# Key sums ahead of the routing, q's transpose ahead of the gates, three place steps a piece: one table of orders changed in a one-core kernel

## The chip, the core and the metric

The program runs on one core of a Trainium2 chip. The metric is the device time of one execution in microseconds (us), as the median of several. Five engines work side by side, each through its own queue in order: TensorE (PE in the profile: matmuls and transposes; PEld are its weight loads), VectorE (DVE), ScalarE (ACT), GpSimd (POOL) and SyncE (SP, which here issues most DMAs).

## What is computed

Attention with keys and values averaged over eight neighbours, then a mixture of experts in two levels, where each token goes to one of 4 x 4 experts:

```
k_p = k.reshape(B, H, Sp, pool, D).mean(axis=3)        # B, H, S, D = 8, 8, 576, 64; pool 8
v_p = v.reshape(B, H, Sp, pool, D).mean(axis=3)
attn = softmax(scale * q @ k_p^T); x = attn @ v_p      # x: 4608 tokens of 512
...
g_idx = np.argmax(x @ w_group, axis=1)                 # group of a token
e_idx = np.argmax(xg @ w_expert[g], axis=1)            # expert in the group
h = np.maximum(xg[mask_e] @ w1[g, e], 0.0)
out[tok_idx] = combined[:, None] * (h @ w2[g, e])      # combined: product of the two softmax weights
```

With the inputs given, seven of the eight batches send all 576 tokens to one expert; batch 5 sends 20 tokens elsewhere.

## The kernel before

The kernel takes the batches b = 0 to 7 one after the other. In the body of batch b, TensorE runs the expert (class `Moe`, `m` in the plans) on batch b: 16 pieces `m.up:f:half` (12 matmuls each, line L532; relu on ScalarE into `ht`, L534; the low-order part `m.upd` on VectorE, L539), then 14 pieces `m.down` of 8 matmuls (L553, L563), whose results ScalarE scales into `y` and stores. All 576 tokens go to the batch's main expert, the one with most tokens. Every float32 operand is used as a high and a low part, so each weight is split: ScalarE casts it (L517), GpSimd, or VectorE where the plan says `:v`, subtracts (L518).

Between these pieces the body does the attention of batch b+1 (`n`, class `Att`), and the start of batch b+2 (`x`): loads of k, v and q, key sums `kr` (L208, two of them), the sum of the rest `rr` (L214), `kb` and `krz` on ScalarE (L226, L227), which TensorE transposes in `kt` (L263, L268); q's transpose on VectorE `qb` (L285); scores `sc` (L291). The sums of v are three folds on GpSimd, `vr` (L230 to L232), then `vmain`: a cast (L245) and four activations (L249) on ScalarE and a subtraction on GpSimd (L246). Loads of k and v share three buffers, so v's second load (`load_v:1`, L176) needs the first key sum done. The bodies 1 to 6 follow the plan STEADY; `x` exists in the bodies 1 to 5. FIRST is the body of batch 0, LAST that of batch 7.

The routing (`n.rt`, `n.route`, `n.main_expert`) turns x into logits `lt` (L371, copied by ScalarE in two halves, L372), transposes them (L379), and finds the expert of each token in 16 short VectorE instructions (L382 to L406) that end in the one-hot `oh`. TensorE counts it (L412), and the expert with most tokens goes to a SyncE register, which the next weight loads use (L510). `gates` (L469 to L483) makes the tokens' weights, `keep_x` (L488 to L494) stores x to DRAM if a token of the batch is left over.

Left-over tokens (class `Left`, `l`) are done at the end in blocks of 32: `place` yields 18 steps that give each a place (`l.step` runs the next one; L621 to L656), `which` finds the block's batch and expert (L663 to L673), `slots` and `rows` its tokens (L678 to L703), `fetch_x`, `fetch_a`, `fetch_b` load x and the weights, `turn` transposes x, `gather`, `back`, `up`, `hback` and `down` do the expert. The first block stands in LAST between the pieces of batch 7; further ones would be done by the loop `block` after it.

What sets the order: a plan is a string of pieces, run from left to right. TensorE, SyncE and VectorE execute in the order of the plan (`MANUAL`; in START all five engines do); the order on ScalarE and GpSimd is set by the framework's planner, from its own model of durations, so a plan that is rearranged can reorder these two as well.

Of the kernel before, what the change touches and what calls it, by code (L numbers as in the profile page):

```python
# [13 lines left out]
ALU = mybir.AluOpType  # L14
# [11 lines left out]
CH = [(0, 128), (128, 128), (256, 128), (384, 128), (512, 64)]  # L26
# [39 lines left out]
x.load_qb:2 x.load_qb:3 x.load_v:0 m.up:6:0 m.upd:6:0 m.split:2:3 m.up:6:1 m.upd:6:1 n.px_:4 n.pm:4 n.pxd:4 n.pmd:4 m.up:7:0 m.upd:7:0  # L66
m.up:7:1 m.upd:7:1 n.av:0:0:256 n.avd:0:0:256 n.av:1:0:256 n.avd:1:0:256 n.av:2:0:256 n.avd:2:0:256 n.av:3:0:256 n.avd:3:0:256
n.av:0:256:320 n.avd:0:256:320 n.av:1:256:320 n.avd:1:256:320 n.av:2:256:320 n.avd:2:256:320 n.av:3:256:320 n.avd:3:256:320 n.rt:0:256
m.down:0 n.rt:256:320 m.down:1 n.route m.down:2 m.down:3 n.main_expert w.load:1:0 w.load:1:1 w.load:1:2 w.load:1:3 m.down:4 x.kr:0 x.kr:1
x.rr x.rcopy x.kb x.load_v:1 m.down:5 n.gates n.keep_x m.down:6 x.vr:0 x.vr:1 m.down:7 w.split:1:0 w.load:2:0 x.kt x.qb:0 m.down:8 m.down:9  # L70
w.split:1:1 w.load:2:1 x.sc:0 x.mx:0 x.sb:0 x.qb:1 m.down:10 x.vmain x.vrem m.down:11 x.su_:0 x.nm:0:p m.down:12 m.down:13
"""
LAST = """
m.up:0:0 m.upd:0:0 m.split:1:2 m.load:2:2 l.step l.step m.up:0:1 m.upd:0:1 l.step l.step m.up:1:0 m.upd:1:0 m.split:1:3 m.load:2:3 l.step
l.xtiles l.step m.up:1:1 m.upd:1:1 l.step l.step m.up:2:0 m.upd:2:0 m.split:2:0 l.step l.step m.up:2:1 m.upd:2:1 l.step l.step m.up:3:0 m.upd:3:0
m.split:2:1:v l.step l.step m.up:3:1 m.upd:3:1 l.step l.step m.up:4:0 m.upd:4:0 l.step l.step m.up:4:1 m.upd:4:1 m.split:2:2 l.step l.step
m.up:5:0 m.upd:5:0 l.tiles l.which l.fetch_x l.fetch_a:1 l.fetch_b:1 m.up:5:1 m.upd:5:1 m.up:6:0 m.upd:6:0 m.split:2:3 m.up:6:1 m.upd:6:1
m.up:7:0 m.upd:7:0 l.slots m.up:7:1 m.upd:7:1 m.down:0 m.down:1 l.rows m.down:2 m.down:12 m.down:13 m.down:3 l.turn:0 l.turn:2
l.turn:1 m.down:4 l.turn:3 l.turn:4 l.next_ l.fetch_x m.down:5 l.gather m.down:6 l.back m.down:7 l.up l.fetch_a m.down:8 l.hback l.slots m.down:9
l.down l.rows l.fetch_b m.down:10 m.down:11  # L80
"""
MANUAL = [{ET.PE, ET.SP, ET.DVE, ET.Activation, ET.Pool}, {ET.PE, ET.SP, ET.DVE}, {ET.PE, ET.SP, ET.DVE}]

# [2 lines left out]
def attn_moe(ctx: ExitStack, tc: tile.TileContext, q, k, v, wg, we, w1, w2, out):  # L86
    nc = tc.nc
# [485 lines left out]
    class Left:  # L573
# [151 lines left out]
        def fetch_b(s, first=None):  # L725
            for j in range(4):
                nc.sync.dma_start(out=s.wb[j], in_=w2v[bass.ds(s.re, 1), :, 2 * j:2 * j + 2, :].rearrange("o p k f -> p (o k) f"),
                                  **({} if first else dict(cond=s.some)))

        def turn(s, c):  # L730

            if s.xr is None:
                s.xr = xp.tile([128, 2, 4, S], F32, name="xt").rearrange("p i g s -> p (i g s)")[:, 0:NC * DM].rearrange("p (c x) -> p c x", c=NC)
            o, n = CH[c]
            ps = ps_t.tile([128, 512], F32, name="tp")
            (nc.gpsimd if c % 2 else nc.vector).tensor_tensor(
                out=s.xh[0][:, :, o:o + n], in0=s.xh[0][:, :, o:o + n], in1=s.xh[1][:, :, o:o + n], op=ALU.add)
# [51 lines left out]
            s.which()  # L789

        def block(s):
            for c in range(NC):
                s.turn(c)
            s.next_()
            s.fetch_x()
            s.gather()
            s.back()
            s.up()
            s.fetch_a()
            s.slots()  # L800
            s.rows()
            s.hback()
            s.down()
            s.fetch_b()
# [67 lines left out]
```

## Time and profile before

| | us |
|---|---|
| median of 3 runs (632.47 to 637.88) | 632.96 |
| the profiled execution, whole / its span | 632.83 / 631.1 |
| TensorE busy in the span | 592.0 |
| VectorE / ScalarE / GpSimd busy | 428.3 / 282.4 / 254.4 |
| TensorE's granted clock, mean (1.00 is 2.4 GHz, .50 is 1.2 GHz) | 0.989 |

A row of a timeline gives the start, the duration, the engine, the line, the operation, output<-inputs by the program's names, the partitions x elements, how many were merged (xcount), and in brackets how long the engine was idle before it and what released it. A duration includes time in which the instruction was held. Lines are those of the kernel before; in the changed kernel the lines from about L730 on stand 3 or 4 further down.

### The profile page before, as it was taken

To read this page: it belongs to the slowest core of one execution; us is meant where nothing else is said; L and a number is where in the kernel's file an instruction comes from. 1 tells how busy PE (TensorE), PEld (TensorE's weight loads), DVE (VectorE), ACT (ScalarE), POOL (GpSimd) and SP (SyncE) were. 2 spreads that over 40 slices of the span, in tenths; PEclk is the share of its full clock that TensorE was granted. 3 is DMA by queue.
4 is the path that set the end of the run, shared out by engine and by line. 5 is a ranking of instruction groups with operands and counts; after the bars stand their busy time and mean duration, and the time that the engine had idled before them with its cause. 6 is when DMAs were issued, how large, how long until landed. Compare 5 with 4: busy or idle time off the path is not lost.

```text
span 631.1 us, 10875 instructions
## 1 busy us (share of the span) xinstructions
PE 592.0 (94%) x3851; PEld 526.9 (83%) x3851; DVE 428.3 (68%) x1002; ACT 282.4 (45%) x585; POOL 254.4 (40%) x255
## 2 busy tenths in 40 slices
PE   6969999999998999899998999899998999998996
PEld 6858887799977998699977998689976998898864
DVE  5877997889565874869575874849656784258321
ACT  3545544465426543374426543364426543253111
POOL 3025535057207550475207560466307652343100
PEclk8989999999999999999999999999999999998999
DMA  6565407356235450654235550693316200630921
GB/s 183 121 210 111 153 35 158 99 200 161 62 103 201 159 110 17 209 192 93 61 110 193 159 110 17 238 311 75 81 65 238 76 1 2 217 125 10 371 81 38
DMA packets 118760, 81.30 MB, mean 129 GB/s; under 512 B 76326, under 2 KB 95270, under 8 KB 118320
## 3 DMA queue, kind: packets, MB, share of 16 engines
q1 hardware_dynamic: 112656, 70.83, 38.5%
q10 hardware_dynamic: 6016, 9.70, 4.1%
q8 instruction: 32, 0.52, 0.3%
q14 instruction: 24, 0.20, 0.1%
q0 software_dynamic: 32, 0.04, 0.0%
HBM read 75.01 MB, written 28.38 MB: 164 GB/s over the span
## 4 chain that ended last, share of the span: by engine, by line
PE 70%; DVE 12%; DMA 11%; SPq 3%; issue 2%; ACT 1%; POOL 0%; DVEq 0%; ACTq 0%; POOLq 0%
PE mm L532 28%; PE mm L553 19%; DMA kv<-in_v_dram 7%; PE tp L358 5%; PE sc L291 5%; PE mm L563 4%; DMA sw<-in_moe_w_dram 3%; PE tp L371 2%; PE tp L343 2%; SPq L510 1%; PE tp L331 1%; DVE kp L208 1%; DMA rp<-rp 1%; DVE ht L539 1%; DVE kv L643 1%
## 5 line engine op out<-in xcount | busy, mean ns | idle before, releaser
L532 PE MATMUL mm<-xt,w 128*128 128x256 f32 (+1 forms) x1536 | 226.0, 302 | 6.8 <-DVE ht L539 2.8
L532 PEld LDWEIGHTS mm<-xt,w 128*128 128x128 f32 x1536 | 210.0, 191 | 10.5 <-issue 4.5
L518 POOL TENSOR_TENSOR w<-sw,w 128x1024 fp32r<-128x1024 f32 x54 | 132.3, 2467 | 150.6 <-ACT w L517 146.7
L553 PE MATMUL mm<-w,ht 128*128 128x512 f32 x768 | 187.5, 395 | 0.0
L553 PEld LDWEIGHTS mm<-w,ht 128*128 128x128 f32 x768 | 140.7, 188 | 29.0 <-issue 0.6
L534 ACT ACTIVATE ht<-mm 128x256 fp32r<-128x256 f32 (+1 forms) x128 | 52.3, 409 | 110.5 <-PE mm L532 109.4
L539 DVE SCALAR_TENSOR_TENSOR ht<-mm,ht 128x256 fp32r<-128x256 f32 (+1 forms) x192 | 60.6, 344 | 31.3 <-ACT ht L534 31.2
L517 ACT CAST w<-sw 128x1024 fp32r<-128x1024 f32 x64 | 65.4, 1045 | 22.5 <-DMA sw<-in_moe_w_dram 12.4
L320 POOL TENSOR_TENSOR px<-p,su 128x96 f32<-128x96 f32 (+1 forms) x72 | 24.6, 362 | 82.9 <-DVE su L312 40.1
L291 PE MATMUL sc<-kT,qT 128*128 128x144 f32 (+1 forms) x320 | 46.7, 289 | 6.9 <-DVE qT L285 6.9
L291 PEld LDWEIGHTS sc<-kT,qT 128*128 128x128 f32 (+1 forms) x320 | 41.2, 180 | 10.7 <-issue 10.3
L558 ACT ACTIVATE y<-mm,gm 128x512 f32<-128x512 f32 x32 | 21.9, 686 | 57.3 <-PE mm L553 57.3
L324 POOL TENSOR_TENSOR p<-p,su 128x576 f32<-128x576 f32 (+1 forms) x36 | 41.4, 1151 | 2.7
L569 DVE TENSOR_TENSOR y<-mm,y 64x512 f32<-64x512 f32 x8 | 5.5, 683 | 47.8 <-ACT y L568 47.8
L310 DVE TENSOR_REDUCE su<-p 128x8 f32<-128x576 f32 (+1 forms) x40 | 29.9, 747 | 10.8 <-ACT p L305 10.3
L298 DVE TENSOR_REDUCE mx<-sc 128x8 f32<-128x576 f32 (+1 forms) x40 | 29.9, 748 | 9.1 <-PE sc L291 8.5
L363 DVE TENSOR_TENSOR xt<-tp,xt 128x320 fp32r<-128x320 f32 (+2 forms) x68 | 29.3, 437 | 8.0 <-ACT xt L359 6.2
L359 ACT CAST xt<-tp 128x320 fp32r<-128x320 f32 (+2 forms) x68 | 26.2, 385 | 17.1 <-PE tp L358 15.1
L208 DVE TENSOR_REDUCE kp<-kv 128x128 f32<-128x1024 f32 x16 | 31.1, 1978 | 3.0 <-DMA kv<-in_k_dram 3.0
L304 DVE TENSOR_TENSOR p<-sc,mx 128x576 f32<-128x576 f32 (+1 forms) x40 | 30.2, 754 | 3.3
L305 ACT ACTIVATE p<-p 128x576 f32<-128x576 f32 (+1 forms) x40 | 27.3, 683 | 10.8 <-DVE p L304 10.0
L563 PE MATMUL mm<-w,ht 128*128 128x512 f32 x128 | 30.3, 389 | 0.0
(206 smaller groups left out, 751.1 us busy)
## 6 DMA issues: line engine op xcount, KB each, us to landing
sw<-in_moe_w_dram SPq DMA_DIRECT2D x72, 512.0 KB
xscr<-xt SPq DMA_DIRECT2D x8, 2304.0 KB
kv<-in_k_dram SPq DMA_DIRECT2D x16, 512.0 KB
kv<-in_v_dram SPq DMA_DIRECT2D x16, 512.0 KB
out_dram<-y ACTq DMA_DIRECT2D x32, 256.0 KB
q<-in_q_dram SPq DMA_DIRECT2D x112, 72.0 KB
kv<-in_moe_w_dram SPq DMA_DIRECT2D x6, 512.0 KB
ph<-xscr SPq DMA_DIRECT2D x2, 1152.0 KB
```

The lines of the kernel that those rows point to most:

```text
L208: red(out=s.kp[:, 2 * u:2 * u + 2, :], in_=s.k[u].rearrange("p g (j d) -> p g d j", j=8), axis=AX.X, op=ALU.add)
L291: nc.tensor.matmul(ps[0:n, g // 2, 144 * (g % 2):144 * (g % 2) + 144], lhsT=s.qT[c][:, g, 0:n], rhs=s.kT[:, g, :], start=(g % 2 == 0), sto ...
L304: tt(out=p[0:n], in0=scv, in1=mx[0:n].unsqueeze(3).broadcast_to([n, 2, 4, SP]), op=ALU.subtract)
L324: eng.tensor_tensor(out=p[0:n], in0=p[0:n], in1=su[0:n].unsqueeze(3).broadcast_to([n, 2, 4, SP]), op=ALU.mult)
L358: nc.tensor.matmul(ps[:, 0:n], lhsT=flat(l[:, g]), rhs=r, start=(i == 0), stop=(i == len(ops) - 1))
L517: nc.scalar.copy(out=wh, in_=raw)
L518: (nc.vector if eng == "v" else nc.gpsimd).tensor_tensor(out=wl, in0=raw, in1=wh.bitcast(F32), op=ALU.subtract)
L532: nc.tensor.matmul(ps[:, 0:n], lhsT=l[:, kc, fs], rhs=xt[:, r, kc, sl], start=(kc == 0 and i == 0), stop=(kc == 3 and i == 2))
L534: nc.scalar.activation(out=ht[:, sl], in_=ps[:, 0:n], func=AF.Relu)
L539: stt(out=ht[:, at:at + hi - lo], in0=ps[:, lo - o:hi - o], scalar=0.0, in1=ht[:, lo:hi].bitcast(F32), op0=ALU.max, op1=ALU.subtract)
L553: nc.tensor.matmul(ps, lhsT=s.ht[f][:, 640 * l + o:640 * l + o + 128], rhs=s.w[2, f // 2][r][:, f % 2, :], start=(i == 0), stop=(i == 23))
L563: nc.tensor.matmul(ps, lhsT=s.ht[f][:, 512:640], rhs=s.w[2, f // 2][r][:, f % 2, :], start=(i == 0), stop=(i == 15))
```

## The change

In the plan STEADY five pieces move: `x.kr:0 x.kr:1 x.load_v:1` from after `m.down:4` to ahead of `m.down:1` and `n.route`, and `x.qb:0` from after `x.kt` to ahead of `n.gates`. In LAST three place steps instead of two stand between two pieces, so they are through after piece 2:1 instead of 4:0; `l.tiles l.which l.fetch_x l.fetch_a:1 l.fetch_b:1` come ahead of piece 4:0 instead of after 5:0; the sums of x's two parts, a half of what was `turn`, become `whole` and stand in a row ahead of all `turn`s; the second `l.rows` goes out of LAST and to the head of the loop's body.

```diff
 STEADY
-m.down:0 n.rt:256:320 m.down:1 n.route m.down:2 m.down:3 n.main_expert w.load:1:0 w.load:1:1 w.load:1:2 w.load:1:3 m.down:4 x.kr:0 x.kr:1
-x.rr x.rcopy x.kb x.load_v:1 m.down:5 n.gates n.keep_x m.down:6 x.vr:0 x.vr:1 m.down:7 w.split:1:0 w.load:2:0 x.kt x.qb:0 m.down:8 m.down:9
+m.down:0 n.rt:256:320 x.kr:0 x.kr:1 x.load_v:1 m.down:1 n.route m.down:2 m.down:3 n.main_expert w.load:1:0 w.load:1:1 w.load:1:2 w.load:1:3
+m.down:4 x.rr x.rcopy x.kb m.down:5 x.qb:0 n.gates n.keep_x m.down:6 x.vr:0 x.vr:1 m.down:7 w.split:1:0 w.load:2:0 x.kt m.down:8 m.down:9
 LAST
-m.up:0:0 m.upd:0:0 m.split:1:2 m.load:2:2 l.step l.step m.up:0:1 m.upd:0:1 l.step l.step m.up:1:0 m.upd:1:0 m.split:1:3 m.load:2:3 l.step
...
+m.up:0:0 m.upd:0:0 m.split:1:2 m.load:2:2 l.step l.step l.step m.up:0:1 m.upd:0:1 l.step l.step l.step m.up:1:0 m.upd:1:0 m.split:1:3 m.load:2:3
...
+l.step l.step l.step m.up:3:0 m.upd:3:0 m.split:2:1:v m.up:3:1 m.upd:3:1 l.tiles l.which l.fetch_x l.fetch_a:1 l.fetch_b:1 m.up:4:0 m.upd:4:0
...
+m.up:7:0 m.upd:7:0 l.slots m.up:7:1 m.upd:7:1 m.down:0 m.down:1 l.rows m.down:2 m.down:12 m.down:13 m.down:3 l.whole:0 l.whole:1
+l.whole:2 l.whole:3 l.whole:4 l.turn:0 l.turn:2 l.turn:1 m.down:4 l.turn:3 l.turn:4 l.next_ l.fetch_x m.down:5 l.gather m.down:6 l.back m.down:7 l.up l.fetch_a m.down:8 l.hback l.slots m.down:9
-l.down l.rows l.fetch_b m.down:10 m.down:11
+l.down l.fetch_b m.down:10 m.down:11

+        def whole(s, c):
+            o, n = CH[c]
+            (nc.gpsimd if c % 2 else nc.vector).tensor_tensor(
+                out=s.xh[0][:, :, o:o + n], in0=s.xh[0][:, :, o:o + n], in1=s.xh[1][:, :, o:o + n], op=ALU.add)
         def turn(s, c):
...
-            (nc.gpsimd if c % 2 else nc.vector).tensor_tensor(
-                out=s.xh[0][:, :, o:o + n], in0=s.xh[0][:, :, o:o + n], in1=s.xh[1][:, :, o:o + n], op=ALU.add)
         def block(s):
+            s.rows()
             for c in range(NC):
+                s.whole(c)
                 s.turn(c)
...
-            s.rows()
             s.hback()
```

How the order of instructions moves, at three places. First VectorE in a steady body, from the last `xt` to the scores: two pieces of the difference, without the 20 rows of routing and election between them (`lg` are the logits, `kp` the key sums, `rp` the sum of the rest, `sg` and `se` the start of the gates).

```order
 L363 TENSOR_TENSOR xt<-tp,xt 128x256 x4
 L363 TENSOR_TENSOR xt<-tp,xt 128x320 x4
+L208 TENSOR_REDUCE kp<-kv 128x128 x2
 L382 TENSOR_REDUCE lg_89<-tp 128x80
...
 L431 TENSOR_SCALAR moh<-cr,ct 128x16
-L208 TENSOR_REDUCE kp<-kv 128x128 x2
 L214 TENSOR_REDUCE rp<-rem 64x128
+L285 STREAM_TRANSPOSE qT<-q 128x512
 L472 TENSOR_REDUCE sg<-dg 128x5
```

The key sums now stand between `xt` and the routing, and q's transpose between the sum of the rest and the gates; it stood behind the whole of gates and `keep_x`.

Second, ScalarE in the same stretch, from the first copy of `lt`: before, then of the change. The planner made this order.

```order
L372 COPY lt<-tp 40x256
L372 COPY lt<-tp 40x320
L469 ACTIVATE dg<-dg 128x20
L558 ACTIVATE y<-mm,gm 128x512
L559 DMA out_dram<-y 128x512
L469 ACTIVATE de<-de 128x20
L558 ACTIVATE y<-mm,gm 128x512
L226 ACTIVATE kb<-kp,sel 128x4x64 x2
```

```order
L372 COPY lt<-tp 40x256
L226 ACTIVATE kb<-kp,sel 128x4x64 x2
L372 COPY lt<-tp 40x320
L245 CAST kp<-vp 128x256
L249 ACTIVATE vmh<-kp,sel 128x4x64 x2
L249 ACTIVATE vml<-vp,sel 128x4x64 x2
L469 ACTIVATE dg<-dg 128x20
L558 ACTIVATE y<-mm,gm 128x512
```

`kb` now stands ahead of the second copy of `lt`, and the cast and activations of v's sums ahead of the gates' exponentials (`dg`, `de`) and of the first `y`. On GpSimd, in the same way, the second set of folds and the subtraction now stand ahead of the two weights:

```order
-L518 TENSOR_TENSOR w<-sw,w 128x1024 x2
 L230 TENSOR_TENSOR kv<-kv 128x2x256
-L255 TENSOR_TENSOR rp<-rp,rh 32x128
 L231 TENSOR_TENSOR kv<-kv 128x2x128
 L232 TENSOR_TENSOR vp<-kv 128x128
 L246 TENSOR_TENSOR vp<-vp,kp 128x256
+L518 TENSOR_TENSOR w<-sw,w 128x1024
+L255 TENSOR_TENSOR rp<-rp,rh 32x128
+L518 TENSOR_TENSOR w<-sw,w 128x1024
```

Third, VectorE in LAST, from the update of piece 3:0 to `which` (L663 on): before, then of the change (L643 to L656 are the last place steps, L518 is the weight that VectorE subtracts).

```order
L539 SCALAR_TENSOR_TENSOR ht<-mm,ht 128x256
L518 TENSOR_TENSOR w<-sw,w 128x1024
L643 SCALAR_TENSOR_TENSOR kv<-kv 128x8x16 x2
L539 SCALAR_TENSOR_TENSOR ht<-mm,ht 128x256
L539 SCALAR_TENSOR_TENSOR ht<-mm,ht 128x64
L643 SCALAR_TENSOR_TENSOR kv<-kv 128x8x16 x2
L539 SCALAR_TENSOR_TENSOR ht<-mm,ht 128x256
L645 SCALAR_TENSOR_TENSOR kv<-kv,loh 128x640
```

```order
L656 CAST niti<-kT 128x1
L539 SCALAR_TENSOR_TENSOR ht<-mm,ht 128x256
L518 TENSOR_TENSOR w<-sw,w 128x1024
L539 SCALAR_TENSOR_TENSOR ht<-mm,ht 128x256
L539 SCALAR_TENSOR_TENSOR ht<-mm,ht 128x64
L663 TENSOR_SCALAR kb<-cum,it 128x128
L664 TENSOR_REDUCE kT<-kb 128x1
L665 TENSOR_SCALAR kT<-kT 128x1
```

All place steps are now ahead of the update of piece 3:0, and `which` follows that of 3:1. ScalarE's casts of the last two weights move as well, by the planner, from behind the relu of piece 3:0 to behind that of 4:0.

## Rows read from the trace of the kernel before

**Rows 1.** The page: each engine's busy time in us, its share of the span, its instructions.

```profile
PE 592.0 (94%) x3851; PEld 526.9 (83%) x3851; DVE 428.3 (68%) x1002; ACT 282.4 (45%) x585; POOL 254.4 (40%) x255
```

**Rows 2.** The waits of TensorE over the whole span: who waited <- for whom, us in total, times, the longest.

```profile
PE sc L291 <- DVE qT L285: 6.9, 5, 1.6
PE tp L268 <- ACT krz L227: 5.6, 6, 1.0
...
PE mm L532 <- DVE ht L539: 2.8, 2, 2.5
...
PE mm L532 <- DVE y L569: 1.5, 1, 1.5
PE tp L739 <- DVE gl L787: 1.2, 1, 1.2
```

**Rows 3.** Timeline of TensorE in the body of batch 3: the transposes of the logits and the count.

```profile
318.41 0.48 PE L379 MATMUL tp<-ident,lt 40*128 40x40 f32 x5
...
322.62 0.45 PE L412 MATMUL tp<-oh,ones 128*128 128x80 f32 x2
```

**Rows 4.** Timeline of VectorE in the same body, from the routing to q's transpose; the idle time ahead of L382 begins with the end of the last `xt`.

```profile
318.92 0.33 DVE L382 TENSOR_REDUCE lg<-tp 128x80 f32<-128x160 f32 x1 [5.24 <-PE tp L379]
...
319.59 0.18 DVE L389 TENSOR_TENSOR dg<-lg,m 128x20 f32<-128x20 f32 x1
...
322.32 0.24 DVE L406 TENSOR_TENSOR oh<-og,oe 128x80 f32<-128x80 f32 x1
...
324.27 3.90 DVE L208 TENSOR_REDUCE kp<-kv 128x128 f32<-128x1024 f32 x2
...
330.56 2.31 DVE L474 TENSOR_SCALAR se<-se 128x5 f32<-128x5 f32 x1
...
336.77 0.71 DVE L285 STREAM_TRANSPOSE qT<-q 128x512 f32<-128x512 f32 x1 [0.22 <-DMA kv<-in_v_dram]
```

**Rows 5.** Timeline of ScalarE in the same body: the second copy of `lt`, the second of `kb`'s activations, the first weight's cast.

```profile
316.66 0.42 ACT L372 COPY lt<-tp 40x320 f32<-40x320 f32 x1 [2.62 <-PE tp L371]
...
328.62 0.49 ACT L226 ACTIVATE kb<-kp,sel 128x256 f32<-128x256 f32 x1
329.35 1.05 ACT L517 CAST w<-sw 128x1024 fp32r<-128x1024 f32 x1 [0.24 <-DMA sw<-in_moe_w_dram]
```

**Rows 6.** Timeline of GpSimd in the same body: two weights, the folds of v's second half, the subtraction.

```profile
330.48 4.87 POOL L518 TENSOR_TENSOR w<-sw,w 128x1024 fp32r<-128x1024 f32 x2 [21.37 <-ACT w L517]
336.67 1.27 POOL L230 TENSOR_TENSOR kv<-kv 128x512 f32<-128x512 f32 x1 [1.32 <-DVE lf L492]
...
338.55 0.74 POOL L231 TENSOR_TENSOR kv<-kv 128x256 f32<-128x256 f32 x1
339.36 0.46 POOL L232 TENSOR_TENSOR vp<-kv 128x128 f32<-128x128 f32 x1
340.34 0.74 POOL L246 TENSOR_TENSOR vp<-vp,kp 128x256 f32<-128x256 f32 x1 [0.52 <-ACT kp L245]
```

**Rows 7.** SyncE's DMA issues: the four weight loads of the body of batch 3, and, in the body of batch 4, the store of x, behind which the next weight loads stand.

```profile
325.25 2.65 SPq L510 DMA_DIRECT2D sw<-in_moe_w_dram  x4
...
408.44 0.39 SPq L494 DMA_DIRECT2D xscr<-xt  x1
```

**Rows 8.** The routing in the plan FIRST: GpSimd's subtraction and VectorE's L389 beside it, from the timelines of both engines.

```profile
70.42 0.73 POOL L246 TENSOR_TENSOR vp<-vp,kp 128x256 f32<-128x256 f32 x1 [1.86 <-ACT kp L245]
...
70.75 0.43 DVE L389 TENSOR_TENSOR de<-el,m 128x20 f32<-128x20 f32 x1
```

**Rows 9.** Timeline of ScalarE at the end of the body of batch 4.

```profile
420.36 1.05 ACT L517 CAST w<-sw 128x1024 fp32r<-128x1024 f32 x1 [4.08 <-DMA sw<-in_moe_w_dram]
```

**Rows 10.** Timelines of four engines in LAST, around TensorE's wait.

```profile
575.37 11.34 PE L532 MATMUL mm<-xt,w 128*128 128x256 f32 x72 [2.50 <-DVE ht L539]
...
569.90 4.86 DVE L643 SCALAR_TENSOR_TENSOR kv<-kv 128x128 f32<-128x128 f32 x2
...
567.94 0.38 ACT L534 ACTIVATE ht<-mm 128x256 fp32r<-128x256 f32 x1 [1.00 <-PE mm L532]
...
571.14 0.38 ACT L534 ACTIVATE ht<-mm 128x256 fp32r<-128x256 f32 x1 [0.16 <-PE mm L532]
...
569.34 5.27 POOL L518 TENSOR_TENSOR w<-sw,w 128x1024 fp32r<-128x1024 f32 x2 [7.67 <-ACT w L517]
```

**Rows 11.** Windows: stretch, its length, busy us and instructions of PE, PEld, DVE, ACT and POOL, then TensorE's granted clock, the DMA share, GB/s. The body of batch 3, and two stretches after TensorE's wait in LAST.

```profile
276.00:348.00 72.00, 69.40 (x443) 62.30 (x443) 51.28 (x112) 34.70 (x73) 33.44 (x32) 1.00 0.43 125
...
576.00:580.00 4.00, 4.00 (x20) 4.00 (x20) 3.72 (x15) 0.39 (x1) 0.00 (x0) 0.60 0.00 0
580.00:584.00 4.00, 4.00 (x33) 4.00 (x32) 1.14 (x5) 1.26 (x3) 0.00 (x0) 1.00 0.25 44
```

**Rows 12.** Windows of VectorE alone in LAST: the place steps and updates before the two that were held, and after.

```profile
558.19:569.90 11.71, 9.35 (x31) 1.00 0.27 98
574.68:577.94 3.26, 3.16 (x12) 0.67 0.00 0
```

**Rows 13.** Timelines of GpSimd and VectorE at the end of FIRST: two weights, and `keep_x`.

```profile
132.64 5.09 POOL L518 TENSOR_TENSOR w<-sw,w 128x1024 fp32r<-128x1024 f32 x2 [1.05 <-ACT w L517]
...
135.62 0.15 DVE L492 TENSOR_SCALAR lf<-cm 128x1 int32<-128x1 f32 x1
```

**Rows 14.** The chain of work that ended last: start, us, what; here `rows` in the tail.

```profile
619.96 1.29 PE tp L701 x10
```

More of the change, by code (lines that the diff above doesn't have):

```diff
@@ L73 @@
 LAST = """
-m.up:0:0 m.upd:0:0 m.split:1:2 m.load:2:2 l.step l.step m.up:0:1 m.upd:0:1 l.step l.step m.up:1:0 m.upd:1:0 m.split:1:3 m.load:2:3 l.step
[L75 to L79, printed above, removed]
-l.down l.rows l.fetch_b m.down:10 m.down:11
+m.up:0:0 m.upd:0:0 m.split:1:2 m.load:2:2 l.step l.step l.step m.up:0:1 m.upd:0:1 l.step l.step l.step m.up:1:0 m.upd:1:0 m.split:1:3 m.load:2:3
+l.step l.step l.step l.xtiles m.up:1:1 m.upd:1:1 l.step l.step l.step m.up:2:0 m.upd:2:0 m.split:2:0 l.step l.step l.step m.up:2:1 m.upd:2:1
+l.step l.step l.step m.up:3:0 m.upd:3:0 m.split:2:1:v m.up:3:1 m.upd:3:1 l.tiles l.which l.fetch_x l.fetch_a:1 l.fetch_b:1 m.up:4:0 m.upd:4:0
+m.up:4:1 m.upd:4:1 m.split:2:2 m.up:5:0 m.upd:5:0 m.up:5:1 m.upd:5:1 m.up:6:0 m.upd:6:0 m.split:2:3 m.up:6:1 m.upd:6:1
+m.up:7:0 m.upd:7:0 l.slots m.up:7:1 m.upd:7:1 m.down:0 m.down:1 l.rows m.down:2 m.down:12 m.down:13 m.down:3 l.whole:0 l.whole:1
+l.whole:2 l.whole:3 l.whole:4 l.turn:0 l.turn:2 l.turn:1 m.down:4 l.turn:3 l.turn:4 l.next_ l.fetch_x m.down:5 l.gather m.down:6 l.back m.down:7 l.up l.fetch_a m.down:8 l.hback l.slots m.down:9
+l.down l.fetch_b m.down:10 m.down:11
 """
```

## Prediction

> **What bounds the kernel now.** The page first: TensorE is busy 592.0 us, 94% of the span [rows 1], so the time is TensorE's own work plus its holes, and a change that adds no matmul is worth what it does to the holes. So the next view is the waits of TensorE [rows 2]: five waits for VectorE's transpose of q (6.9 us), six for ScalarE's `krz` (5.6 us, five of them about 1.0 us, one in START), one for VectorE's y (1.5), one of 2.5 for `ht` in the last batch, one of 1.2 for VectorE at the end. The first two kinds stand once in each of the steady bodies 1 to 5, together 12.0 us, 2.4 a body. The body of batch 3 serves as the example.
>
> There VectorE's row [rows 4] has a gap of 5.24 us between the last `xt` (ends 313.68) and the routing (318.92), and then does everything in a string: routing, key sums (324.27, 3.90 us), remainder sum, gates, and only then q's transpose (336.77). `krz` and the transpose are late because of that string. In the gates one instruction of 5 values a partition took 2.31 us: GpSimd was subtracting a weight (330.48, two in 4.87 us) [rows 6], and VectorE's instruction ended when the first of them did.
>
> **What the change does to a steady body.** The two key sums (3.90 us) move into the gap: 313.7 to 317.6, done before the routing needs VectorE. The remainder sum then follows the election directly, and q's transpose stands ahead of the gates. Both old waits go: `krz` and the transpose come more than 2 us ahead of their matmuls even when the routing ends 2 us late. Gain 12.0 us. The gates, now later than the transpose, delay nothing: their results are used in the next body.
>
> But two other things move, and the order of the changed kernel shows them.
>
> First, ScalarE. `kb` (two activations of .49 us) now stands ahead of the copy of the second half of `lt`. It waits for the second key sum (317.6); the copy, which ran at 316.66 [rows 5], would end at 317.6 + 2 x .49 + .42 = 319.0; rows of one engine overlap a little, so I take 318.9. TensorE transposes `lt` from 318.41 on, five in .48 us [rows 3]; the third, due near 318.6, waits to some .05 after the copy: **.37 us**. Bounds: 0 (if TensorE gets there later) to .5.
>
> Second, GpSimd. v's second load now follows the first key sum (315.68), not the weights. Its nearest duration is the first weight load of the same 512 KB: issued 325.25, used by ScalarE at 329.35, 4.1 us [rows 5, 7]; v1 so lands near 319.8. GpSimd's three folds (1.27, .74, .46 us) and, .52 behind them for ScalarE's cast, the subtraction (.74) [rows 6] run from there, not at 336 to 341 as before. That is exactly under the routing, whose instructions mostly read two operands in SBUF. Such a one has been caught in FIRST: L389, .18 us elsewhere, took .43 when GpSimd's L246 was running, and ended with it [rows 4, 8]. Stepping through the routing, which starts at 319.3, with one VectorE instruction let through between two of GpSimd's: L389 waits from 320.0 for the first fold's end (321.1, 1.1 us), L391 for the second (.6), L395 for the third (.15), a later one for the subtraction (.1). The one-hot `oh` comes 1.95 us late. TensorE's count matmul has no slack: before, `oh` ended at 322.56 and the matmul started at 322.62 [rows 3, 4]. So TensorE waits **1.95 us** at the count. Bounds by the same steps: v1 landing 2 us sooner gives .8; at the worst moment 2.7; landing over 7 us after its issue, 0.
>
> What else queues behind these waits: on ScalarE the cast of v's sum stands ahead of the first exponential, the first y and `krz`'s copies, so these wait for the folds until 324.8; the y's buffer is wanted by the tenth `down` step after 334, the exponentials by the gates after 329, `krz` by TensorE after 332. On SyncE the load of v1 waits for the first key sum, and behind it stands the election's register, read after 324. On GpSimd the folds are through 6 us before the first weight. All of that is hidden.
>
> Sum per body 2.32 us of new waits against 2.4 of old: over five bodies 12.0 - 11.6 = **+0.4 us**.
>
> The body of batch 4 also had the 1.5 us wait for y. ScalarE sat 4.08 us for a weight cast (420.36) whose load stands behind the store of `xt` (408.44) [rows 7, 9]. With the key sums gone from behind the election and the gates not held by GpSimd, the gates end near 332 instead of 336.5 (in the example's times), that store is issued some 4 us earlier, and the load, queued behind it, comes at least 2 us sooner: **+1.5**.
>
> **Last batch.** Before: GpSimd's two subtractions (569.34, 5.27 us) held two `L643` steps (4.86 us), the `ht` update queued behind them came late, TensorE waited 2.5 us [rows 10]. And its clock: granted 1.00 before, .60 in the 4 us after the restart, where 20 matmuls ran for 33 in the next 4 us: another 13/33 of 4 = 1.6 us [rows 11]. Cost 4.1 us.
> Now three steps a piece. VectorE's work from 558.19 up to `which` is 9.35 + 3.16 busy [rows 12] plus the two held steps at some .25 less one update of some .4, estimates both: 12.6; adding .6 for the second piece's matmuls, which VectorE must await, and .3 for a GpSimd weight still running, the end is near 571.7; adding the steps one by one I get 572.2. ScalarE's casts of the last two weights now follow the relu at 571.14; GpSimd started 1.40 us after the relu ahead of it (567.94 to 569.34), so it starts at 572.5 [rows 10]. All steps are through by then, and L663 of `which` is just in front. Of the rest of `which`, the one-value instructions are not held (L492, .15 us inside the second half of 132.64 + 5.09 [rows 13]); the two-value cast may be, and I count it as held to 574.9. The `ht` update of piece 4:0 then ends near 575.7; TensorE wants its buffer for piece 5:1, at 574.3 (575.37 - 2.50 = 572.87 for the start of 5:0, and some 1.45 for its twelve matmuls at the full clock). Wait 1.4, below the 1.6 that left the clock alone in the steady bodies [rows 2, 11]. Gain 4.1 - 1.4 = **+2.7**. Bounds: +4.1 if the cast isn't held, -1.4 if L663 is (then both subtractions hold `which`, the wait is 3.9 and the clock goes as well).
>
> Here a rule speaks against the row. The Trainium skill (VectorE: DVE Perf Modes, What auto-detection actually checks) gives an instruction with one source the second port if source and destination lie in SBUF and their outermost dimensions are both even or equal, which one value meets; another page of the Trainium skill (SBUF — State Buffer, Who interferes with whom) has such an instruction blocked by a GpSimd instruction that came first. By these two `which` would be held twice, and the sum would be 4.1 less. L492 was not held, so the row decides.
>
> The x fetch goes out about 5 us earlier, so GpSimd's half of `whole` may meet `slots` and delay `rows` by 0 to .6: taken at **-.3**. VectorE's own sums stand behind y of the 64-row chunk as before and start no sooner.
>
> **The end.** The fifth sum ahead of the transposes ends the 1.2 us wait [rows 2]; `rows` (1.29 us in the chain [rows 14]) is gone from the tail, where TensorE's work runs to the last output: **+2.5**. The loop body changes too, but 20 leftover tokens make one block, which the plan itself does: the loop runs zero times.
>
> **Sum.** .4 + 1.5 + 2.7 - .3 + 2.5 = 6.8 us. The profiled execution took 632.83 (span 631.1), the median is 632.96, so 632.83 - 6.8 = **626.0**.
>
> **Rivals.**
> - *The routing isn't held* (v1 lands after it, as before, when the folds began 8.8 us after the weights' issues, 327.90 to 336.67 [rows 6, 7]; or short folds hold little): only .37 a body is left, steady +10.1 instead of +0.4: 616.3; with the lower bound .8, 620.2. For it: nothing but L389 shows a short GpSimd instruction holding a routing instruction. Against: that one, and an empty queue at 316. Chance .15.
> - *The clock goes with the count wait, and the end is slower than before.* Waits of 1.6 us left TensorE at 2.4 GHz, 2.5 us sent it to 1.2 GHz [rows 2, 11]; 1.95, with .37 a few us ahead, lies between. The place is the count matmul, the price 1.6 us a body: 627.6 with one body, 632.4 with four, 634.0 with five, slower than before from the fifth on (6.8/1.6 = 4.2). Chance .22. Against it: the body of batch 3 ran at 1.00 with its two waits [rows 11].
> - *`which` meets both subtractions*, because the steps end later or because one-value instructions are held too: 2.7 becomes -1.4, 626.0 + 4.1 = 630.1. For it: the margin is .3 to .8 us on a string of 30 instructions. Against: L492. The Trainium skill's rule above would give this time. Chance .16.
> - Something not listed, slower by over 1%: .05.
>
> **Numbers.** My forecast has .42; its own range is 624 to 628 (bounds of the .37, the 1.95 and the cast). A difference of about 1% (626.6 and 639.3 as limits) is what a measurement of this kernel tells from none. Faster by over 1%: the first rival's .15 and a good half of the forecast's own, .26: .41. Slower: .05. Within: the rest, .54. The range leaves out the first rival's low end and the clock in all five bodies: 619.0 to 632.5.
>
> **What would show it.** In the changed profile: no TensorE wait at `krz` and the q transpose; new waits of some .4 at L379 and 2 at L412; L389 and L391 of the routing long, ending with L230 and L231; ScalarE's second `lt` copy after `kb`; the y wait of batch 4 gone; a wait near 1.4 in the last batch with the clock at 1.00; no 1.2 at the last transposes. Wrong if the routing's instructions stay at .2 us, or if the granted clock falls in steady bodies.

## The result, and the profile after

The changed kernel takes **615.12 us** (median of 4 runs, 614.83 to 615.41) against 632.72 (median of 4, 632.30 to 637.88) for the kernel before beside it: ratio .9704, 95% interval .9653 to .9754. The forecast was 626.0 with a range from 619.0; the time lies below both. It is near what the prediction gave its first rival, that the routing isn't held (616.3, chance .15, outside the stated range), though the reason is another than the rival's. The profiled execution has a span of 612.7 us where the one before had 631.1.

First the page, part 1 as in [rows 1], then the waits of TensorE over the span as in [rows 2].

```profile
PE 589.0 (96%) x3841; PEld 525.6 (86%) x3841; DVE 404.8 (66%) x1000; ACT 281.8 (46%) x585; POOL 253.8 (41%) x255
```

```profile
PE tp L331 <- DVE px L320: 3.2, 2, 2.0
PE tp L263 <- ACT kb L226: 2.9, 1, 2.9
PE mm L532 <- DVE ht L539: 1.6, 2, 1.3
PE tp L278 <- DMA q<-in_q_dram: 1.4, 1, 1.4
```

Busy time fell by 3.0 us: 1.3 for the `rows` of the tail, and about the 1.6 that the clock cost in the last batch. The other 15.4 us of the span are idle time of TensorE. Of the five waits of [rows 2] four are gone: q's transpose, `krz` (five of the six), the y of batch 4, the `gl` at the last transposes. The first, second and fourth lines here are from the first 100 us, START and FIRST, which the change doesn't touch. What is left of the old list is the wait for `ht`, 1.3 instead of 2.5 us. The body of batch 3, in the same window as in [rows 11], shows TensorE busy 71.93 of 72 us where it was 69.40:

```profile
276.00:348.00 72.00, 71.93 (x464) 65.14 (x463) 48.95 (x119) 35.74 (x75) 34.43 (x34) 1.00 0.48 139
```

That body again by timelines: TensorE (answers to [rows 3]), VectorE ([rows 4]), ScalarE ([rows 5]), GpSimd ([rows 6]) and SyncE's issue of v's second load. An issue's row starts when SyncE lets it go.

```profile
314.45 0.72 PE L379 MATMUL tp<-ident,lt 40*128 40x40 f32 x5
...
318.91 0.45 PE L412 MATMUL tp<-oh,ones 128*128 128x80 f32 x2
...
309.63 3.88 DVE L208 TENSOR_REDUCE kp<-kv 128x128 f32<-128x1024 f32 x2
...
315.88 0.18 DVE L389 TENSOR_TENSOR dg<-lg,m 128x20 f32<-128x20 f32 x1
...
318.61 0.24 DVE L406 TENSOR_TENSOR oh<-og,oe 128x80 f32<-128x80 f32 x1
...
313.55 0.91 ACT L226 ACTIVATE kb<-kp,sel 128x256 f32<-128x256 f32 x2 [3.47 <-DVE kp L208]
314.37 0.40 ACT L372 COPY lt<-tp 40x320 f32<-40x320 f32 x1
...
304.49 0.46 POOL L232 TENSOR_TENSOR vp<-kv 128x128 f32<-128x128 f32 x1
308.61 1.30 POOL L230 TENSOR_TENSOR kv<-kv 128x512 f32<-128x512 f32 x1 [3.65 <-DMA kv<-in_v_dram]
...
310.80 0.46 POOL L232 TENSOR_TENSOR vp<-kv 128x128 f32<-128x128 f32 x1
315.15 0.74 POOL L246 TENSOR_TENSOR vp<-vp,kp 128x256 f32<-128x256 f32 x1 [3.89 <-ACT kp L245]
...
304.98 0.38 SPq L176 DMA_DIRECT2D kv<-in_v_dram  x1
```

And SyncE's own wait for that load, from the list of SyncE's waits (as in [rows 2], for this engine):

```profile
SPq L176 <- POOL vp L232: 15.0, 6, 2.7
```

Read it from the last row of the timelines. The load went out at 304.98, .03 us after the end of the fold L232 of v's *first* half (304.49 + .46), and 4.65 us *before* the first key sum began (309.63). The same holds in each of the five steady bodies: the load leaves within .03 us of that fold's end, and five of the six waits listed are these. So it got the buffer of v's first half, not that of k's; the sentence in the section on the kernel before, by which this load needs the first key sum done, is wrong in the same way. Its folds ran from 308.61 to 311.26 and were over 4 us before the routing. Only the subtraction L246 lies beside the routing, and it holds nothing there: the instructions under it are reductions, as short as before, and the first one with two sources, L389, starts as it ends and takes its .18 us. The one-hot `oh` ended at 318.85 and the count began at 318.91: no wait. What the prediction had of ScalarE is there: `kb` waits for the key sums, the second copy of `lt` ends at 314.77, and the five transposes L379 take .72 us instead of .48.

The last batch (answers to [rows 10], then two windows for the clock):

```profile
562.46 8.43 PE L532 MATMUL mm<-xt,w 128*128 128x320 f32 x60 [1.28 <-DVE ht L539]
...
559.64 0.15 DVE L666 TENSOR_SCALAR kT<-kT 128x1 f32<-128x1 f32 x1
559.83 2.00 DVE L668 CAST ki<-kT 128x2 int32<-128x2 f32 x1
561.86 0.15 DVE L669 TENSOR_SCALAR ki<-ki 128x1 int32<-128x1 int32 x1
...
559.41 4.72 POOL L518 TENSOR_TENSOR w<-sw,w 128x1024 fp32r<-128x1024 f32 x2 [10.89 <-ACT w L517]
```

```profile
561.00:565.00 4.00, 2.72 (x20) 2.54 (x19) 2.17 (x8) 0.82 (x2) 3.14 (x2) 1.00 0.00 0
565.00:569.00 4.00, 4.00 (x33) 4.00 (x32) 1.53 (x5) 0.82 (x2) 0.00 (x0) 1.00 0.97 325
```

All place steps are through before GpSimd's two subtractions begin at 559.41. Of `which` only the cast of two values, L668, is held: 2.00 us, to the end of the first subtraction. The one-value instructions ahead of it and behind it run in .15 us under the same two. The updates behind it come late, TensorE waits 1.28 us, and the clock stays at 1.00.

### The profile page after: what moved, and what is told of

Read it like the earlier page. It is cut to its first block, busy times and chain, and to the rows that moved or that the text cites. A ratio compares the mean times of both kernels' runs of the same rounds, so it can differ in the third digit from the quotient of the medians.

```text
span 612.7 us, 10857 instructions
## 1 busy us (share of the span) xinstructions
PE 589.0 (96%) x3841; PEld 525.6 (86%) x3841; DVE 404.8 (66%) x1000; ACT 281.8 (46%) x585; POOL 253.8 (41%) x255
## 4 chain that ended last, share of the span: by engine, by line
PE 78%; DVE 13%; DMA 3%; ACT 2%; issue 2%; SPq 1%; POOL 0%; DVEq 0%; POOLq 0%
PE mm L532 28%; PE mm L553 26%; PE sc L291 5%; PE tp L358 5%; PE mm L563 5%; DVE kp L208 3%; PE tp L343 2%; DMA kv<-in_v_dram 2%; DMA sw<-in_moe_w_dram 1%; DVE ht L539 1%; PE tp L331 1%; ACT kb L226 1%; PE tp L371 1%; DVE px L320 1%; DVE xt L363 1%
## 5 line engine op out<-in xcount | busy, mean ns | idle before, releaser
L553 PE MATMUL mm<-w,ht 128*128 128x512 f32 x768 | 187.7, 396 | 0.0
L518 POOL TENSOR_TENSOR w<-sw,w 128x1024 fp32r<-128x1024 f32 x54 | 131.7, 2456 | 95.2 <-ACT w L517 90.9
L517 ACT CAST w<-sw 128x1024 fp32r<-128x1024 f32 x64 | 65.5, 1048 | 23.2 <-DMA sw<-in_moe_w_dram 13.4
L320 POOL TENSOR_TENSOR px<-p,su 128x96 f32<-128x96 f32 (+1 forms) x72 | 24.5, 360 | 96.3 <-DVE su L312 53.2
L291 PEld LDWEIGHTS sc<-kT,qT 128*128 128x128 f32 (+1 forms) x320 | 42.6, 184 | 2.3 <-issue 1.6
L324 POOL TENSOR_TENSOR p<-p,su 128x576 f32<-128x576 f32 (+1 forms) x36 | 41.4, 1149 | 2.8
L230 POOL TENSOR_TENSOR kv<-kv 128x512 f32<-128x512 f32 x13 | 16.8, 1292 | 32.8 <-DMA kv<-in_v_dram 32.3
```

Source lines behind the costliest of these rows:

```text
L291: nc.tensor.matmul(ps[0:n, g // 2, 144 * (g % 2):144 * (g % 2) + 144], lhsT=s.qT[c][:, g, 0:n], rhs=s.kT[:, g, :], start=(g % 2 == 0), sto ...
L324: eng.tensor_tensor(out=p[0:n], in0=p[0:n], in1=su[0:n].unsqueeze(3).broadcast_to([n, 2, 4, SP]), op=ALU.mult)
L517: nc.scalar.copy(out=wh, in_=raw)
L518: (nc.vector if eng == "v" else nc.gpsimd).tensor_tensor(out=wl, in0=raw, in1=wh.bitcast(F32), op=ALU.subtract)
L553: nc.tensor.matmul(ps, lhsT=s.ht[f][:, 640 * l + o:640 * l + o + 128], rhs=s.w[2, f // 2][r][:, f % 2, :], start=(i == 0), stop=(i == 23))
```

## The experiments

Three groups of kernels, e1 to e4, e5 to e8 and e9 to e12, ran each on one chip, beside the kernel before. That kernel took 634.22, 638.51 and 634.76 us (medians) there. Many of these kernels have executions some 4 us over their lowest; in the profiled ones a collision at the end of FIRST goes with it (last section). Where a small difference matters, the lowest executions are compared.

**The steady part alone, the last part alone.** STEADY of the change with LAST of before, and the reverse.

> The plan STEADY of the change with the plan LAST and the functions of before. Theory A (the saving in the steady bodies is 2.4 us a body of old waits less .3 for the second copy of lt, and 1.5 for y in the body of batch 4): 12.0 - 1.5 + 1.5 = 12.0 us faster than before, 620.8, and in LAST the 2.5 us wait with the clock at 1.2 GHz stands as before. Rival B (the steady bodies are worth the +1.9 us that the prediction gave them, .4 and 1.5, and the last batch gave the rest): 631.

> The plan LAST and the functions of the change with the plan STEADY of before. Theory A: 2.8 us in the last batch (old wait and clock loss 4.1, new wait 1.3) and 2.5 at the end, 5.3 together: 627.4; the wait for ht is 1.2 to 1.4 us and the clock stays at 2.4 GHz behind it. Rival B: the last batch carries nearly all of the 17.6 us: 617.

Measured: e1 619.7 us, ratio .9782 (.9720 to .9844), 14.5 us under the 634.22 beside it; e2 629.43, ratio .9920 (.9887 to .9953), 4.8 under. The two add up to 19.3; e4 below, the changed kernel but for one harmless move, lies 19.2 under on that chip. So the steady bodies carry three quarters of the gain; B falls in both. By the lowest executions (632.18 before, 619.25 and 627.94) the two are worth 12.9 and 4.2, near A's 12.0 and 5.3. In e1 the waits for `ht` (2.5) and `gl` (1.2) stand as before, in e2 those for the transpose and `krz` (7.0 and 5.2 us), while its wait for `ht` is the 1.3 of the changed kernel, with the clock at 1.00 behind it. e2 lies 2.0 over A's figure, but the kernel before beside it lies 1.5 over the one that A started from; in the profiled execution the wait for the y of batch 4 is .8 longer, 2.3 us.

But one expectation of e1 failed: the clock. TensorE waits the same 2.50 us at the same place, and no window behind it shows the lower clock:

```profile
560.00:564.00 4.00, 1.50 (x12) 1.26 (x11) 4.00 (x7) 0.44 (x1) 2.11 (x1) 1.00 0.00 0
564.00:568.00 4.00, 4.00 (x32) 3.95 (x31) 3.73 (x18) 0.99 (x3) 0.00 (x0) 1.00 0.00 0
```

**The load where the prediction had it.** The three buffers get names, so that each load's buffer is fixed; the tiles that the left-over tokens take from the same buffers get names too (not shown).

```diff
+        NAMES = {0: ["kva", "kvb", "kvb", "kvc"], 2: ["kvb", "kvc", "kva", "kvb"]}
+        buf = lambda s, i: s.NAMES.get(s.b, ["kva", "kvb", "kvc", "kva"])[i]
...
-            t = s.k[u] = sk.tile([128, 2, 512], F32, name="kv")
+            t = s.k[u] = sk.tile([128, 2, 512], F32, name=s.buf(u), bufs=1)
...
-            t = s.v[u] = sk.tile([128, 2, 512], F32, name="kv")
+            t = s.v[u] = sk.tile([128, 2, 512], F32, name=s.buf(2 + u), bufs=1)
```

> The changed kernel with the three buffers of k and v given out by name, so that v's second load takes the buffer of the first half of k, as the prediction had it, instead of the buffer of the first half of v; nothing else is changed. Theory H (the prediction's price was right for a load that waits for the first key sum): the load lands near the start of the routing, the folds L230 to L232 hold L389, L391 and their like, and TensorE waits .8 to 2.7 us at the count in each of five bodies; 615.1 + 4 to 13, by the prediction's 1.95 a body 624.9. Theory N (short folds don't hold the routing, or land behind it): no wait at the count over .3 us, 614.5 to 616.5. If the count's wait is near 2 us the granted clock may fall as well, which would add up to 1.6 a body.

Measured: 622.49 us, 7.4 over the changed kernel, and as much over e4 (615.07, below) on the same chip. Theory H. First the wait in the list of TensorE's waits and that of SyncE for the load, then the body of batch 3 (its times are some 8 us later, since earlier waits are in them): the issue, GpSimd, VectorE.

```profile
PE tp L412 <- DVE oh L406: 7.4, 5, 1.7
SPq L176 <- DVE kp L208: 63.3, 5, 13.3
```

```profile
319.95 0.39 SPq L176 DMA_DIRECT2D kva<-in_v_dram  x1
...
323.63 1.29 POOL L230 TENSOR_TENSOR kva<-kva 128x512 f32<-128x512 f32 x1 [10.25 <-DMA kva<-in_v_dram]
325.00 0.78 POOL L231 TENSOR_TENSOR kva<-kva 128x256 f32<-128x256 f32 x1
325.85 0.49 POOL L232 TENSOR_TENSOR vp<-kva 128x128 f32<-128x128 f32 x1
326.86 0.73 POOL L246 TENSOR_TENSOR vp<-vp,kp 128x256 f32<-128x256 f32 x1 [0.52 <-ACT kp L245]
...
324.17 0.78 DVE L389 TENSOR_TENSOR dg<-lg,m 128x20 f32<-128x20 f32 x1
...
325.20 0.17 DVE L393 TENSOR_REDUCE m<-rg 128x5 f32<-128x20 f32 x1
325.41 0.39 DVE L395 TENSOR_TENSOR og<-rg,m 128x20 f32<-128x20 f32 x1
...
326.06 0.39 DVE L401 TENSOR_TENSOR es<-lg,og 128x80 f32<-128x80 f32 x1
...
327.01 0.61 DVE L389 TENSOR_TENSOR de<-el,m 128x20 f32<-128x20 f32 x1
```

Now the load leaves at 319.95, just behind the first key sum, and lands 3.7 us later. Each GpSimd instruction holds one two-source instruction of the routing, which ends with it or just behind it: L389 at 324.95 with the first fold (324.92), L395 at 325.80 with the second (325.78), L401 .11 behind the third (326.45 and 326.34), the second L389 with the subtraction (327.62 and 327.59). The reduction L393, inside the second fold, isn't held. The five waits at the count are 7.4 us, the whole of the difference between the medians (the profiled execution, 625.7 us of span, has the collision of the last section on top, 2.8 us). The granted clock stayed at 1.00 around the wait of 1.28 here (windows 322 to 334 of that trace), and over all five bodies (146 to 600), whose waits at the count are 1.28 to 1.66 us.

**Which of the moves pays.** e4 puts `x.qb:0` back behind `x.kt`; e5 moves it alone; e8 puts the load alone back.

```diff
 e4
-m.down:5 x.qb:0 n.gates ... x.kt m.down:8
+m.down:5 n.gates ... x.kt x.qb:0 m.down:8
 e5
-n.rt:256:320 x.kr:0 x.kr:1 x.load_v:1 m.down:1 ... m.down:4 x.rr x.rcopy x.kb m.down:5
+n.rt:256:320 m.down:1 ... m.down:4 x.kr:0 x.kr:1 x.rr x.rcopy x.kb x.load_v:1 m.down:5
 e8
-x.kr:0 x.kr:1 x.load_v:1 m.down:1 ... x.kb m.down:5
+x.kr:0 x.kr:1 m.down:1 ... x.kb x.load_v:1 m.down:5
```

> The changed kernel with q's transpose back in its old place, behind the gates and x's transposes; the key sums and v's second load stay ahead of the routing. Theory A (the transpose was late because of the string, and the 3.9 us of key sums in that string were enough): the transpose ends 3 us or more before its matmuls, no wait for it, 615 as with both moves. Theory Q (q's own move is what pays 1.4 a body): the wait at L291 is back, 6.9 us in five, 622.

> The changed kernel with both key sums and v's second load back in their old place, behind the election; q's transpose alone stands ahead of the gates. Theory A (the transpose needs only to be out from behind the gates, krz needs the 3.9 us of sums out of the string): the wait at L291 is gone, krz keeps its 1.0 us in each of five bodies, the .3 at L379 is not there; 615.1 + 5.0 - 1.5 = 618.6, and up to 1.5 more if the wait for y in the body of batch 4 is back. Rival: krz's wait goes too (it hung on the gates), 613.6.

> The changed kernel with v's second load alone back in its old place, behind the weight loads in SyncE's queue; sums and transpose as changed. Theory A (the load's move pays nothing by itself: the folds only have to keep off the routing and off the gates): GpSimd does the two weights first, the folds after them, when the gates are through; 614.5 to 616. Rival (the folds or v's cast come so late that ScalarE or TensorE waits for v, or a y behind them does): 617 to 620.

Measured: e4 615.07 us, as with both moves; no wait for the transpose. The key sums, moved together with v's load, cure both waits: with 3.9 us out of the string, and the gates no longer held, the transpose (in its old place, in the body of batch 3; first row) ends at 325.48, and its matmuls start at 330.85.

```profile
324.77 0.71 DVE L285 STREAM_TRANSPOSE qT<-q 128x512 f32<-128x512 f32 x1 [0.22 <-DMA sw<-in_moe_w_dram]
...
330.85 1.14 PE L291 MATMUL sc<-kT,qT 128*128 128x144 f32 x8
```

e5 622.25 (lowest 620.79, .7 over A's upper figure): the transpose's wait is gone, `krz` keeps its waits (line below), and TensorE still waits 1.0 for the y of batch 4.

```profile
PE tp L268 <- ACT krz L227: 5.6, 6, 1.0
```

e8 615.94 (lowest 615.05): the folds run behind the two weights, as A has it, and the load's move is worth nothing measurable. The key sums alone, without either of the other moves, were not run.

**The two waits that the change brought.** e6 puts the second key sum back; e7 and e11 move `which`; e9 joins e6 and a third place for `which`; e10 is the changed kernel, for the comparison.

```diff
 e6, e9
-n.rt:256:320 x.kr:0 x.kr:1 x.load_v:1 m.down:1 ... m.down:4 x.rr
+n.rt:256:320 x.kr:0 x.load_v:1 m.down:1 ... m.down:4 x.kr:1 x.rr
 e7
-l.step l.step l.step m.up:3:0 ... l.tiles l.which l.fetch_x
+l.step l.step l.step l.tiles l.which m.up:3:0 ... l.fetch_x
 e9
-m.up:3:0 m.upd:3:0 m.split:2:1:v ... l.tiles l.which l.fetch_x
+m.up:3:0 m.upd:3:0 l.tiles l.which m.split:2:1:v ... l.fetch_x
 e11
-m.upd:3:1 l.tiles l.which l.fetch_x l.fetch_a:1 l.fetch_b:1 m.up:4:0 ... m.up:5:0 m.upd:5:0 m.up:5:1
+m.upd:3:1 m.up:4:0 ... m.up:5:0 m.upd:5:0 l.tiles l.which l.fetch_x l.fetch_a:1 l.fetch_b:1 m.up:5:1
```

> The changed kernel with the second key sum back behind the election; the first and v's load stay ahead of the routing, q's transpose ahead of the gates. ScalarE's kb then stands behind the second copy of lt. Theory A (the .3 at L379 is the copy waiting behind kb): that wait is gone in five bodies; the string behind the election is 1.95 us longer than in the changed kernel and 1.95 shorter than before, so krz, 1.0 late before, is in time: 615.1 - 1.5 = 613.6. Rival (krz or the transpose has less room than that): up to 1 us a body back, 618.

> The changed kernel with which (and the naming of its tiles) right behind the last place step, ahead of the update of piece 3:0 and of VectorE's weight, so that its cast L668 is through before GpSimd's two subtractions begin. Theory A (the wait of 1.28 us in the last batch is this cast held by the first of them): the wait is gone and nothing else moves, 615.1 - 1.3 = 613.8. Rival (VectorE's weight L518 or the updates, now later, are held in its place): a wait of 1 us or more stays, 615 to 616.

> The second key sum back behind the election, as in e6_second_sum_back, and which between the update of piece 3:0 and VectorE's weight: the update isn't pushed back by which, as in e7_which_early where .71 us came of that, and the cast L668 is still through before GpSimd's subtractions. Theory A (the two waits that the change brought are independent of each other and of the rest): both go, 1.2 in the steady bodies and 1.3 in the last batch, so 2.5 us under the changed kernel that runs beside it. Rival: VectorE's weight, now .1 to .7 us under GpSimd's first, is held or holds it, and a wait of 1 us or more for ht stays in the last batch: 1.2 under it.

> The changed kernel itself, for a measure on the same chip as the other three: 615 where that chip is as the first one was, or some us more; without disturbance at the start of the second body, no TensorE wait over .3 us between 100 and 560 us.

> The changed kernel with which, the naming of its tiles and the fetches back behind piece 5:0; the place steps stay three a piece. Theory A (the wait of 1.28 us comes of which being early enough to meet GpSimd, not of the steps): L668 runs after both subtractions in .2 us, no wait for ht, 1.3 us under the changed kernel; the fetches go out some 3 us later and still land before the sums need them. Rival (which or the updates meet the second subtraction, or the later fetch makes TensorE wait at the transposes): as the changed kernel, or 1 us over it.

Measured, in us: e6 617.22 (613.39 to 619.25), e7 616.47 (614.83 to 618.30), both too scattered to tell 1 us; their traces do. In e6 the copy of `lt` stands ahead of `kb` again, the five transposes take their old .48 us, and no wait at `krz` or q's transpose is there, so A's mechanism holds:

```profile
319.20 0.48 PE L379 MATMUL tp<-ident,lt 40*128 40x40 f32 x5
```

In e7 the cast L668 takes .17 us, but a wait of .71 comes in the place of the 1.28: the update of piece 3:0 now stands behind `which`. Neither theory as written; not quite half of the 1.28 is had.

e9 to e12 ran six times each beside one another, and the three lowest executions of each are: e10 614.56, 614.66, 615.35; e9 612.77, 613.29, 613.85; e11 613.65, 613.72, 613.76. By their means e9 is 1.6 and e11 1.1 us under the changed kernel. The medians over all six (614.32, 615.49 and 615.54 for e9, e10, e11) and the ratios (.9686, .9709, .9697, each with some .003 to .004 to both sides) can't tell them apart. e9 was to give 2.5: its trace still has .64 at 564.58, since `which` (1.4 us) and the weight (1.2) now both stand between two updates. So A holds for `lt` and in half for `ht`; the rival's 1 us isn't there either. In e10's trace TensorE has no wait over .3 us between 100 and 560 us, as expected. In e11 the wait is gone altogether, though not for A's reason: `which` meets the *second* subtraction and its first instruction is held 2.29 us (first row; the second is GpSimd), but the updates that TensorE wants next are ahead of it by then.

```profile
566.62 2.29 DVE L663 TENSOR_SCALAR kb<-cum,it 128x128 f32<-128x128 f32 x1
...
564.05 4.76 POOL L518 TENSOR_TENSOR w<-sw,w 128x1024 fp32r<-128x1024 f32 x2 [10.89 <-ACT w L517]
```

e9 is the fastest of all kernels here by its lowest executions, and it stands under the kernel before by its interval; that it beats the changed kernel isn't settled by an interval.

**The tail.**

```diff
-l.whole:0 l.whole:1 l.whole:2 l.whole:3 l.whole:4 l.turn:0 l.turn:2 l.turn:1 m.down:4 l.turn:3 l.turn:4
+l.whole:0 l.turn:0 l.whole:2 l.turn:2 l.whole:1 l.turn:1 m.down:4 l.whole:3 l.turn:3 l.whole:4 l.turn:4
...
-l.down l.fetch_b
+l.down l.rows l.fetch_b
```

> The changed kernel with each sum of x's two parts directly ahead of its own transposes, as before, and the second rows back in LAST. Theory A (the tail's terms were 1.2 for the wait and 1.3 for rows): both are back, 2.5 us over the changed kernel. Rival (rows runs in time in which the last outputs are under way anyway, or the wait goes elsewhere): 1.2 over it, or 0.

Measured: 619.08 us; the three lowest 617.05, 617.50, 617.63, by their mean 2.5 over e10's. Theory A: the wait of 1.2 us at the last transposes is back in the list of waits, and what is left, 1.3, is the size of the `rows` of [rows 14]. The two came back together, so the shares are read from the list and by subtraction, not from a run each.

```profile
PE tp L742 <- DVE gl L790: 1.2, 1, 1.2
```

## Why the prediction was wrong

**The step that failed** is "v's second load now follows the first key sum (315.68), not the weights". The load did stop standing behind the weights, but it never waited for the key sum. The prediction took it that the fourth load of a body has the first one's buffer; the code, which asks for one of three, doesn't say so. It got the one that came free first. The trace of before showed which that would be: the folds of v's first half were through at 309.1 there, 6.5 us before the first key sum was to end. The last of them, on GpSimd's timeline of the kernel before, in the body of batch 3:

```profile
308.65 0.46 POOL L232 TENSOR_TENSOR vp<-kv 128x128 f32<-128x128 f32 x1
```

From this one step came the landing at 319.8, the folds beside the routing and the 1.95 us at each count, 9.8 us in five bodies; without it the prediction's own sum gives the first rival's 616.3.

**The price behind the wrong premise was right in kind.** e3 made the premise true: the routing was held by exactly these four GpSimd instructions (three folds and the subtraction), TensorE waited 1.3 to 1.7 us a body where 1.95 was stated (with .8 to 2.7 as bounds), and the time rose by 7.4 us. The first rival's second reason, that short folds may hold little, is wrong; its first, that the folds don't lie beside the routing, is right, but they came before it, not after.

**Old waits, +12.0.** Right: 6.9 for q's transpose and 5.0 for `krz` are gone. That the sums would do both (e4), so that q's own move adds nothing to them, was not foreseen: the prediction gave the two moves one sum. By itself q's move cures its own wait and leaves `krz` late (e5).

**.37 at L379.** Right in mechanism, too large: .24 a body (.72 for .48), 1.2 in all instead of 1.85.

**+1.5 for y in batch 4.** Right: not in the list after.

**Last batch, +2.7.** The new wait was 1.28 for a stated 1.4, and for the stated reason, the held cast of two values. That one-value instructions aren't held is what the prediction took from L492; that the two-value cast is held was its assumption, and it came out. By the prediction's reading of the Trainium skill (VectorE: DVE Perf Modes, What auto-detection actually checks; SBUF — State Buffer, Who interferes with whom) the one-value ones would be held as well. L666 ran in .15 us beside a GpSimd instruction that had come first, so here the measurement decides against that reading. The first of these sections of the Trainium skill speaks of the "outermost non-unit dims", and one value a partition has no such dimension; whether that is the reason no run here shows. The clock's 1.6 us came back in this pair of profiled executions, but e1, with the same 2.50 us wait at 1.00, shows that this wait alone doesn't bring it; as a sure term it was too much.

**-.3 at `rows`, +2.5 in the tail.** No wait over .25 us is at `rows` after; the tail gave 2.5 (e12).

**The sum, put right.** Idle and clock gone: 11.9 + 1.5 + 1.2 (for `ht`) + 1.6 (clock) + 2.5 - 1.2 (L379) = 17.5 us, against 17.6 between the medians and 18.4 between the two spans; .9 of the spans' difference I don't assign. Since the clock's 1.6 belongs to one pair of executions, the match with the medians is in part luck.

**The clock rival.** Its place, the count's wait, didn't come to be. In e3, where it did with 1.3 to 1.7 us, the clock stayed at 1.00 in all five bodies; a wait of 1.95 there was not run.

## What to carry to other kernels

Before a moved load is costed, find out which buffer it will get: look in the trace for the reader that frees one first, and, once the changed kernel has run, for what the load waited for; a pool with several buffers needn't go round in turn, and the code's order doesn't tell. One assumption of this kind decided between 0 and 7 us here. And when two moves cure two waits, ask whether the first one already takes both late steps out of the same string.

## What the runs showed that was not expected

**A collision that a few tenths of a us decide.** At the end of FIRST, which no kernel here changes, VectorE's L324 and L488 both read two operands while GpSimd subtracts two weights. The rows of two executions, e10 (span 612.5) and then e9 (616.2, with TensorE's wait); in each VectorE's rows stand above GpSimd's:

```profile
132.98 0.76 DVE L324 TENSOR_TENSOR p<-p,su 128x576 f32<-128x576 f32 x1
133.66 2.36 DVE L488 TENSOR_TENSOR cr<-cnt,moh 128x16 f32<-128x16 f32 x1
...
133.25 5.10 POOL L518 TENSOR_TENSOR w<-sw,w 128x1024 fp32r<-128x1024 f32 x2 [1.03 <-ACT w L517]
```

```profile
140.73 1.53 PE L532 MATMUL mm<-xt,w 128*128 128x256 f32 x9 [1.97 <-DVE y L569]
...
134.53 2.87 DVE L324 TENSOR_TENSOR p<-p,su 128x576 f32<-128x576 f32 x1
137.33 2.35 DVE L488 TENSOR_TENSOR cr<-cnt,moh 128x16 f32<-128x16 f32 x1
...
134.40 5.24 POOL L518 TENSOR_TENSOR w<-sw,w 128x1024 fp32r<-128x1024 f32 x2 [0.63 <-ACT w L517]
```

In e10 L324 starts .27 us ahead of GpSimd and runs its .76; only L488 is held. In e9 GpSimd is .13 us ahead, L324 is held to the end of the first subtraction and L488 to that of the second, the y behind them is late, and TensorE waits 1.97 us. Its clock then falls (window below, granted .71). The Trainium skill (SBUF — State Buffer, Who interferes with whom) says that the order of issue decides who is held; these two traces agree. The same split runs through the profiled executions of the changed kernel and of all twelve: L324 takes .76 us in eight (the changed kernel, e1, e2, e4, e7, e8, e10, e12; ahead of GpSimd's pair by .03 to .29 us), and none of them waits for y there; it takes 2.8 to 2.9 us in the other five (e3, e5, e6, e9, e11), and each waits 1.9 to 2.8 us. In e3, e5 and e6 the pair comes earlier still: the first subtraction holds L320, the instruction ahead of L324 (2.6 us for two, .43 elsewhere), the second holds L324, and L488 goes free.

What parts the two groups stands on ScalarE. VectorE's string waits for a softmax that ScalarE does behind one weight's cast L517, and GpSimd's pair waits for the next cast. These two casts start 3.2 to 3.4 us apart in the eight (128.69 and 132.13 in e10) and 2.8 to 3.0 us in the five (130.24 and 133.27 in e9); in the five both casts wait for the DMA of their weight. Most executions of e9, e11 and e12 fall in two groups 3 to 5 us apart; that this collision is what parts those without a profile too is argued, not shown.

**The clock and the length of a wait.** TensorE fell below 2.4 GHz after 2.50 us in the kernel before [rows 10, 11] and after 1.97 us in e9 (window below; in the same window of e3, e5, e6 and e11, after their waits of 1.9 to 2.8 us, .65, .57, .69 and .78 were granted). It did not after 2.50 us in e1, nor after 1.28 in the changed kernel, nor after five waits of 1.28 to 1.66 in e3. So 2.50 us stands on both sides, and the length of a wait alone doesn't tell.

```profile
140.00:144.00 4.00, 3.27 (x19) 3.26 (x20) 3.90 (x9) 2.37 (x5) 0.00 (x0) 0.71 0.39 87
```
